# Which queue issues which of the first weight rows: two early transfers swapped between SyncE and ScalarE in a two-problem attention kernel

## The chip, the cores and the metric

The kernel runs on one core of a Trainium2 chip. The metric is the device time of one execution in microseconds (us), lower is better. Times are medians of several executions. Five engines matter: TensorE (PE, with its weight loader PEld), VectorE (DVE), ScalarE (ACT), GpSimd (POOL) and SyncE (SP). SyncE and ScalarE both issue memory transfers, each to a queue of its own; the profile calls the transfers of SyncE q1 and those of ScalarE q10.

## The reference

Two independent problems A and B of the same shape, each an attention block with cached keys and values; their outputs are laid side by side.

```python
# x (16,32,1024)  k_cache, v_cache (16,4,512,128)  wq (1024,4096)  wo (4096,1024), all bf16
q = (x @ wq).reshape(B, Sq, Hq, Dh).transpose(0, 2, 1, 3)
k = jnp.repeat(k_cache, rep, axis=1)
v = jnp.repeat(v_cache, rep, axis=1)
p = softmax(jnp.einsum("bhqd,bhkd->bhqk", q, k) * Dh ** -0.5)
o = jnp.einsum("bhqk,bhkd->bhqd", p, v)
out = o.transpose(0, 2, 1, 3).reshape(B, Sq, Hq * Dh) @ wo
```

## The kernel before

Only the opening, some 18 us of it, concerns the change. It computes the first eight heads of q for problem A. The rows of wq come in eight chunks of 128 rows (`dc` 0 to 7); w0 holds them for heads 0 to 7, and NF is 6, so "heads 0 to NF" are the six heads computed first. Chunks 0 and 1 of x come as rows and are transposed by TensorE; the others come by a transposing transfer.

```python
load_x(TT // 2, TT, nc.scalar)                 # half of x's rows, ScalarE
nc.scalar.preload_act_table_set("natural_log_exp_and_others")
load_x(0, TT // 2)                             # the other half, SyncE
load_w0(0, 1, 0, NF // 2)                      # chunk 0, heads 0 to 2, SyncE, 96 KB
load_w0(0, 1, NF // 2, NF)                     # chunk 0, heads 3 to 5, SyncE, 96 KB
load_w0(1, 2, 0, NF, nc.scalar)                # chunk 1, ScalarE, 192 KB
load_x_transposed(2)                           # chunks 2 and 3 of x, SyncE, 256 KB
load_w0(2, 3, 0, NF, nc.scalar)                # chunk 2, ScalarE, 192 KB
load_w0(3, 4, 0, NF)                           # chunk 3, SyncE
...
warm_up(22)                                    # dummy matmuls until x is there
for k, ts in enumerate(((0, TT // 2), (TT // 2, TT))):
    transpose_x(0, *ts, nc.vector.tensor_copy)
    transpose_x(1, *ts, nc.scalar.copy, spare[k])
for ts in ((0, TT // 2), (TT // 2, TT)):
    first_heads(range(0, NF // 2), (0,), *ts)  # six half-width matmuls
first_heads(range(NF // 2, NF), (0,))          # chunk 0, heads 3 to 5
first_heads(range(NF), (1, 2, 3))              # chunks 1, 2, 3
...
```

The prediction counts the chunks from one: its "first chunk" is chunk 0, its "second" chunk 1, its "third" chunk 2. I do the same below.

## Time and profile before

| | kernel before |
|---|---|
| median, three runs at first | 343.48 us |
| span of the profiled execution | 340.8 us |
| TensorE busy | 99% of the span |
| first matmul on the first weights (line 531) | 4.20 us |
| first matmul of the rest (line 301) | 18.45 us |

The page draws the span in 40 slices; a digit is the busy share in tenths, and PEclk is the granted TensorE clock in tenths. This is that part of the page of the kernel before:

```profile
PE   8999999999999999999999999999999999999996
...
PEclk9999999999999999999999999999999999999999
DMA  8999999989996998899999966998449996430001
```

### The profile page before, as it was taken

The page shows a single profiled execution, that of the slowest core. Times are in us where ns is not written, and L with a number is a line of the kernel's source. Part 1 is how long each engine was busy: PE and PEld are TensorE (multiplying, and loading weights), DVE is VectorE, ACT ScalarE, POOL GpSimd, SP SyncE. Part 2 cuts the span into 40 slices and gives each one's busy share as a digit, 9 for nine tenths or more (in the row PEclk, how much of TensorE's full clock was granted, in tenths as well). Part 3 has the DMA queues.
Part 4 walks back from the last instruction along what each step waited for, and adds up shares of the span by engine and source line. Part 5 has one row for each costly group of instructions (what it writes and reads, how often), then busy time and mean ns, then how long its engine had stood idle before and what let it go on. Part 6 is the DMA issues. An engine that isn't in the chain of part 4 may idle for free.

```text
span 340.8 us, 5475 instructions
## 1 busy us (share of the span) xinstructions
PE 336.7 (99%) x2113; PEld 213.0 (62%) x2113; DVE 265.2 (78%) x335; ACT 185.4 (54%) x208; POOL 46.7 (14%) x206
## 2 busy tenths in 40 slices
PE   8999999999999999999999999999999999999996
PEld 5456666666666666666666666666666666666555
DVE  0047988888888898888888898879888888889540
ACT  2067666666757667666645544554554555555110
POOL 0001111011111111110012221222122101111100
PEclk9999999999999999999999999999999999999999
DMA  8999999989996998899999966998449996430001
GB/s 208 297 186 270 287 248 223 188 238 259 312 266 159 241 230 227 214 291 296 317 297 285 239 125 148 344 283 211 125 106 300 355 193 161 105 100 13 17 19 33
DMA packets 128622, 71.70 MB, mean 210 GB/s; under 512 B 76880, under 2 KB 127824, under 8 KB 128592
## 3 DMA queue, kind: packets, MB, share of 16 engines
q1 hardware_dynamic: 127504, 69.68, 84.1%
q0 software_dynamic: 384, 1.05, 0.9%
q10 hardware_dynamic: 704, 0.59, 0.6%
q8 instruction: 17, 0.28, 0.4%
q14 instruction: 13, 0.11, 0.1%
HBM read 50.59 MB, written 2.10 MB: 155 GB/s over the span
## 4 chain that ended last, share of the span: by engine, by line
PE 99%; ACT 0%; issue 0%; ACTq 0%
PE f_ps L320 32%; PE q_ps L301 28%; PE s_ps L357 16%; PE ob L425 16%; PE q_ps L531 4%; PE q_ps L513 1%; PE xT_ps L521 0%; ACT o_sb L329 0%; ACTq L329 0%
## 5 line engine op out<-in xcount | busy, mean ns | idle before, releaser
L365 ACT ACTIVATE p_sb<-s_ps,shift 128x1024 bf16<-128x1024 f32 x128 | 142.7, 1115 | 97.5 <-PE s_ps L357 85.0
L376 DVE TRANSPOSE_TENSOR_REDUCE parts<-p_sb 128x32 f32<-128x1024 bf16 x128 | 158.8, 1240 | 20.9 <-ACT p_sb L365 19.3
L320 PE MATMUL f_ps<-wo_sb,oT 128*128 128x512 bf16 (+1 forms) x544 | 132.3, 366 | 0.0
L301 PE MATMUL q_ps<-xT,wq_sb 128*128 128x512 bf16 x448 | 116.9, 379 | 0.0
L357 PE MATMUL s_ps<-qT,kT 128*128 128x256 bf16 x512 | 76.8, 273 | 0.0
L425 PE MATMUL ob<-p_sb,v_sb 128*128 128x256 bf16 x512 | 76.8, 273 | 0.0
L320 PEld LDWEIGHTS <-oT 128*128 128x128 bf16 x544 | 53.2, 98 | 35.3
L357 PEld LDWEIGHTS <-kT 128*128 128x128 bf16 x512 | 56.9, 113 | 28.3
L301 PEld LDWEIGHTS <-wq_sb 128*128 128x128 bf16 x448 | 43.8, 98 | 32.2
L425 PEld LDWEIGHTS <-v_sb 128*128 128x128 bf16 x512 | 50.1, 98 | 20.0
L447 DVE TENSOR_TENSOR oT<-r,ob 128x512 bf16<-128x512 f32 x64 | 43.9, 686 | 19.9 <-PE ob L425 19.4
L411 DVE STREAM_TRANSPOSE r<-rall 128x512 f32<-128x512 f32 x64 | 44.2, 691 | 1.1
L309 ACT CAST qT<-q_ps 128x512 bf16<-128x512 f32 x56 | 32.7, 583 | 16.5 <-PE q_ps L301 16.5
L394 POOL COPY half<-cs 64x32 f32<-64x32 f32 x32 | 6.5, 204 | 231.4 <-DVE cs L384 231.3
L329 ACT CAST o_sb<-f_ps 128x512 bf16<-128x512 f32 (+1 forms) x17 | 9.5, 559 | 23.6 <-PE f_ps L320 23.6
L531 PE MATMUL q_ps<-xT,w_sb 128*128 128x512 bf16 (+1 forms) x67 | 14.4, 374 | 0.0
L384 DVE TENSOR_REDUCE cs<-parts 128x32 f32<-128x128 f32 x32 | 12.0, 376 | 1.1
L406 DVE RECIPROCAL rall<-sums 128x32 f32<-128x32 f32 x32 | 10.2, 320 | 3.3 <-POOL sums L403 3.3
L553 DVE CAST qT<-q_ps 128x512 bf16<-128x512 f32 x4 | 2.5, 684 | 12.8 <-PE q_ps L531 12.8
L531 PEld LDWEIGHTS <-w_sb 128*128 128x128 bf16 x67 | 6.5, 100 | 7.5 <-DMA w_sb<-in_A_wq_dram 0.3
L553 ACT CAST qT<-q_ps 128x512 bf16<-128x512 f32 x4 | 2.1, 599 | 12.3 <-PE q_ps L531 12.3
L331 POOL DMA_DIRECT2D out_dram<-o_sb x8 | 4.6, 574 | 29.3 <-ACT o_sb L329 29.3
(25 smaller groups left out, 48.2 us busy)
## 6 DMA issues: line engine op xcount, KB each, us to landing
v_sb<-in_A_v_cache_dram SPq DMA_DIRECT2D x16, 512.0 KB, 6.0
wq_sb<-in_B_wq_dram SPq DMA_DIRECT2D x8, 1024.0 KB, 5.8
wo_sb<-in_A_wo_dram SPq DMA_DIRECT2D x8, 1024.0 KB, 7.6
v_sb<-in_B_v_cache_dram SPq DMA_DIRECT2D x16, 512.0 KB, 4.8
wo_sb<-in_B_wo_dram SPq DMA_DIRECT2D x8, 1024.0 KB, 8.5
wq_sb<-in_A_wq_dram SPq DMA_DIRECT2D x5, 1024.0 KB, 6.7
wq_sb<-in_A_wq_dram SPq DMA_DIRECT2D x2, 512.0 KB, 7.3
kT<-in_A_k_cache_dram SPq DMA_TRANSPOSE x64, 4.4
```

The lines of the kernel that those rows point to most:

```text
L301: nc.tensor.matmul(ps[:], lhsT=w[:, dc, (h % 4) * DH:(h % 4 + 1) * DH], rhs=xT[pr][:, dc, :], start=(dc == 0), stop=(dc == DC - 1),)
L309: nc.scalar.copy(out=qT[pr, g][:, :, hl, :], in_=ps[:].rearrange("p (b s) -> p b s", s=SQ),)
L320: nc.tensor.matmul(ps[:, 0:width], lhsT=oT[pr, tt][:, h, :], rhs=wo_tiles[pr, nh, h // REP][:, h % REP, off:off + width], start=(h == 0), ...
L357: nc.tensor.matmul(s_ps[:, c, :], lhsT=kT[:, i % GRP, c, :], rhs=qT[pr, g][:, b, :, :].rearrange("p h s -> p (h s)"), start=True, stop=True,)
L365: nc.scalar.activation(out=p_sb[:], in_=s_ps[:], func=ACTF.Exp, bias=shift[:], scale=SCALE)
L376: nc.vector.tensor_reduce(out=parts[k][:, q, :, :].rearrange("p c h -> p (c h)"), in_=st[i]["p"][:].rearrange("p c (h s) -> p (c h) s", s=SQ),
L384: nc.vector.tensor_reduce(out=cs[:], in_=parts.pop(k)[:].rearrange("p q c h -> p q h c"), axis=AX.X, op=ALU.add,)
L406: nc.vector.reciprocal(out=rall[:, k, :], in_=quad.pop(k)[:])
L411: nc.vector.transpose(out=r[:].rearrange("p n s -> p (n s)"), in_=rall[:, k, o * 2 * REP:(o + 1) * 2 * REP] .unsqueeze(2).to_broadcast([P, ...
L425: nc.tensor.matmul(ob[j][:, q, :], lhsT=v_sb[:, i % GRP, c, :], rhs=st[i]["p"][:, c, :], start=(c == 0), stop=(c == KC - 1),)
L447: nc.vector.tensor_tensor(out=out, in0=rcp.pop(j)[:].rearrange("p (q h) s -> p q h s", h=REP), in1=ob.pop(j)[:].rearrange("p q (h s) -> p ...
L531: nc.tensor.matmul(first_q[h][:, ts], lhsT=w0[dc // HC][:, dc % HC, h * DH:(h + 1) * DH], rhs=xT[0][:, dc, ts], start=(dc == 0 and t0 == 0 ...
```

## The change

Its intent is to bring the first chunk's heads 3 to 5 earlier, as TensorE waits for them. They go to ScalarE's queue as its second transfer, and the second chunk takes their place on SyncE's. The third chunk stays ScalarE's third transfer; only its line in the program moves ahead of the transpose.

```diff
             load_x(0, TT // 2)
             load_w0(0, 1, 0, NF // 2)
-            load_w0(0, 1, NF // 2, NF)
-            load_w0(1, 2, 0, NF, nc.scalar)
+            load_w0(0, 1, NF // 2, NF, nc.scalar)
+            load_w0(1, 2, 0, NF)
+            load_w0(2, 3, 0, NF, nc.scalar)
             load_x_transposed(2)
-            load_w0(2, 3, 0, NF, nc.scalar)
             load_w0(3, 4, 0, NF)
```

## The prediction

> **What bounds the kernel now.** I read the page first, then the chain of waits, the waits of the weight loader, and the timeline and DMA views of the first 20 us.
>
> ```profile
> span 340.8 us, 5475 instructions
> PE 336.7 (99%) x2113; PEld 213.0 (62%) x2113; DVE 265.2 (78%) x335; ACT 185.4 (54%) x208; POOL 46.7 (14%) x206
> ...
> PE 99%; ACT 0%; issue 0%; ACTq 0%
> ```
>
> These are the span, the busy times and the chain that ended last, by engine. TensorE is 99% of that chain. A change that touches neither the number nor the shape of the matmuls can only win from the holes between them, and all of its edit lies before the 10th microsecond. The chain of waits for the first 25 us shows that opening (start, length, what):
>
> ```profile
> 0.93 2.52 PE q_ps L513 x22
> 3.45 0.95 PE xT_ps L521 x8
> 4.40 0.84 PE q_ps L531 x6
> 5.24 0.01 issue
> 5.25 13.36 PE q_ps L531 x61
> 18.61 3.45 PE q_ps L301 x16
> ```
>
> Warm-up matmuls run till x lands, eight transposes follow, then six half-width matmuls (first chunk, heads 0 to 2, two halves) and 61 full-width ones. The waits of the weight loader say where this stretch has holes:
>
> ```profile
> PEld L531 <- DMA w_sb<-in_A_wq_dram: 0.3, 1, 0.3
> PEld L521 <- DMA x_sb<-in_A_x_dram: 0.2, 1, 0.2
> ```
>
> Only the first of them, one wait for a weight transfer, is the target of this change. A loader runs ahead of the matmuls, so its 0.3 us is not TensorE's hole. The timeline of 5.0 to 5.23 us on TensorE gives that:
>
> ```profile
> 4.75 0.49 PE L531 MATMUL q_ps<-xT,w_sb 128*128 128x256 bf16 x3
> ```
>
> Three matmuls of 256 columns start at 4.75 and then 0.11 apart, so the third starts at 4.97 and TensorE could go on at 5.08. The chain has the next one (first chunk, head 3) at 5.25. **The hole is 5.25 - 5.08 = 0.17 us**, 0.05% of the span.
>
> The second thing to read is what follows it. From 5.25 three matmuls of the first chunk (heads 3 to 5) and six of the second come before the third chunk's first. The records place the starts of those nine 0.216 us apart (0.227 once), which makes 5.25 + 9 x 0.216 = 7.19, plus 0.01. The third chunk's first matmul starts at 7.23. It waits 0.03 us for the transposed rows of x (line 468), whose landing the DMA view of 2 to 4 us gives beside the weights' (KB each, us from issue to landing):
>
> ```profile
> w_sb<-in_A_wq_dram ACTq DMA_DIRECT2D x1, 192.0 KB, 4.3
> w_sb<-in_A_wq_dram SPq DMA_DIRECT2D x1, 192.0 KB, 4.4
> w_sb<-in_A_wq_dram SPq DMA_DIRECT2D x1, 96.0 KB, 3.5
> xT<-in_A_x_dram SPq DMA_TRANSPOSE x1, 5.0
> ```
>
> The timeline has the issues at: first chunk heads 0 to 2 on SyncE 1.25, second chunk on ScalarE 1.34, first chunk heads 3 to 5 on SyncE 1.75, third chunk on ScalarE 1.83, transpose on SyncE 2.22, fourth chunk on SyncE 3.60. With the times to landing (exact ones from the semaphore records) they land at 4.16, 5.01, **5.20**, 6.11, **7.19** and 7.96. So two landings hold TensorE, the one at 5.20 and the one at 7.19, and they are in series: the second has been almost met already.
>
> **What the Trainium skill says.** Its page "DMA: Bandwidth & Descriptors", section "Issuing engines are not separate DMA queues", says that transfers started by ScalarE and SyncE end up on the same 16 engines and that a second issuer only saves issue time. The trace agrees: both queues together move 276 GB/s in the stretch 2 to 4 us and 293 in 6 to 8 us with the engines near full, and the packets of the six transfers begin in the order of issue, whichever queue they are on (3.1, 3.4, 3.6 to 3.9, 4.1, 4.7, 6.3 us). So what the change alters is the order of transfers in one common line. The same page, "Queues, rings and completion order", says that an engine with work on two rows takes a packet of each in turn; the trace shows that too, with packets of both queues alternating from 3.4 to 5.6 us. "Perfetto Trace Analysis", section "DMA Instruction — HWDGE (DVE, Sync)", says that the data movement is not in the instruction's profiled window: here an issue lasts 0.43 us and the data lands 3.5 us after it, so I go by landings. "TensorE: Matmul & The Clock Gate", section "Wait — 56ns, not 53.3ns?", gives 215.7 ns between warm 512-column matmuls; the trace has 216 ns, so between the two landings TensorE can't be sped up.
>
> **The change, part by part.** No instruction is added or removed; three issues change their queue or place. The built program shows the same PE, DVE and POOL streams, with two semaphores swapped on TensorE.
>
> 1. *First chunk, heads 3 to 5: from SyncE's third issue to ScalarE's second.* Issued at 1.34 instead of 1.75, 0.41 us earlier, and 192 KB fewer stand ahead of it. Its rate is about 300 GB/s, so 192 KB are 0.64 us. I expect it to land 0.6 to 0.9 us earlier, near 4.4 (5.20 less 0.8, an estimate from these two numbers). Needed at 5.08. **The hole of 0.17 us closes.**
> 2. *Second chunk: from ScalarE's second issue to SyncE's third.* Issued 0.41 us later, with 96 KB more ahead (0.32 us). Where the two overlap on the line the sum of bytes is the same as that which landed at 5.20 before, so I put it at 5.2 to 5.6, the higher value if it shares the engines packet by packet with the third chunk's 192 KB. It is needed at 5.08 + 3 x 0.216 = 5.73. Cost nothing, with 0.1 to 0.5 us to spare.
> 3. *Third chunk: ScalarE's third issue as before*, at about 1.8. It lands between 5.6 and 6.1, and is needed at 5.08 + 9 x 0.216 = 7.02. Cost nothing.
> 4. *The transpose: still SyncE's fourth issue, at about 2.22.* The same bytes stand ahead of it (x, two parts of chunk one, chunks two and three), so I leave its landing at 7.19, with 0.2 us either way since it now follows a larger transfer in its own ring and has less beside it on the other. TensorE now wants it at 7.02 and gets it at 7.19: **a wait of 0.17 + 0.03 = 0.20 us here takes the place of the 0.17 + 0.03 us before**, and the third chunk starts at 7.23 as it did.
> 5. *All that comes after*: issued behind the transpose, in the same order, at the same times. The fourth chunk lands at 7.96 and is wanted at 7.23 + 5 x 0.216 = 8.31 by the loader, so it has 0.35 us to spare.
>
> Sum: -0.17 at 5.08, +0.17 at 7.02, so about 0.0 us. The time stays at the median before, 343.48; I write 343.4, as a transpose landing a little earlier would be paid out in full.
>
> **The rivals.**
> - *The transpose lands earlier too.* It doesn't carry the same work beside it, and if its packets got started before 4.7 us, up to all of the 0.20 us would be won: 343.28. Against it: the same bytes ahead, and in the trace its 1024 packets run in two halves (4.7 to 5.85, 5.9 to 6.4 us), the second starting when the slowest engine has finished the first. Weight packets on the other queue set that, and they are all still there.
> - *The second chunk becomes the wait.* If it shares packet by packet with the third chunk, and both end at 6.0, TensorE waits 0.3 us at 5.73, which then is inside the wait at 7.02 only in part: chunk two would start at 6.03, end at 7.33, 0.1 later than the landing of the transpose, so +0.1 us: 343.6. Against it: SyncE's issue (1.75) is still ahead of ScalarE's third (1.83), and so far packets began in order of issue.
> - *The transpose lands later.* With both big weight transfers alternating, its ring is blocked till about 5.1 instead of 4.7, and its landing slips by up to 0.4: 343.9. For it: SyncE's ring now holds 192 KB rather than 96 KB before the transpose. Against it: the second half then meets no weight packets, and the first half has fewer.
> - *A hole re-throttles TensorE.* The clock record has 1.00 throughout, and holes of 0.2 us were there before. I give it nothing.
>
> **Range and chances.** All mechanisms lie within -0.2 to +0.5 us. The three runs before spread from 342.94 to 343.48, and the profiled execution was another at 342.66, so the spread of measurement (0.8 us) is larger than all of them. Hence 342.7 to 344.0. A change of 2% would be 6.9 us; nothing in the first ten microseconds is that long. Chances: 0.005 faster, 0.99 same, 0.005 slower.
>
> **What would show the steps right or wrong.** In the profile after, the chain of waits should have the first chunk's heads 3 to 5 follow the six half-width matmuls at about 5.08, with no "issue" piece between them, and the loader's wait for w_sb at that place gone (step 1). The second chunk should start within 0.05 us of 5.73 (step 2), the loader showing no wait there. A hole of about 0.2 us should stand before the third chunk's first matmul, put down to the transposed x, with that matmul at 7.2 to 7.3 (step 4). The line 301 matmuls should again start at 18.6, give or take 0.2. I am wrong in the mechanism if they start at 18.4 (the transpose moved forward) or at 18.8 and later (it or the second chunk moved back), and wrong altogether if the time leaves 342.7 to 344.0 while the opening is unchanged, for then something outside it moved.

## The result

| | before | changed |
|---|---|---|
| median of 6 runs | 343.27 us | 342.91 us |
| lowest to highest | 342.94 to 343.48 | 342.55 to 343.21 |
| ratio | | 0.999, 95% interval 0.9977 to 1.0003 |
| span of the profiled execution | 340.8 us | 341.1 us |

A ratio is the mean time of one kernel's runs over that of the other's in the same rounds, so it is not quite the ratio of the medians. Executions over 1.5% slower than the fastest of the same kernel are left out of the means. The interval contains 1: the time is the same. The profiled execution of the changed kernel even has the longer span.

These lines of the changed kernel's page are the span, the busy times and the chain that ended last by engine:

```profile
span 341.1 us, 5436 instructions
...
PE 334.5 (98%) x2074; PEld 212.8 (62%) x2113; DVE 265.4 (78%) x335; ACT 185.3 (54%) x208; POOL 47.0 (14%) x206
...
PE 96%; DMA 2%; issue 1%; ACT 0%; SPq 0%; ACTq 0%
```

Before, TensorE had 99% of the chain; now it has 96%, and transfers have 2%. The matmul count of 2074 against 2113 is no change of work: the loader still has 2113 instructions, and 39 matmul records are missing from this trace. The chain bridges such gaps with pieces of "issue", which explains most of that 1%. The 2% of transfers is real, and the chain of waits in order of time shows where (start, length, what):

```profile
1.75 4.48 DMA w_sb<-in_A_wq_dram
6.23 0.05 issue
6.28 2.33 PE q_ps L531 x10
```

The waits of the loader and of TensorE in the same profile:

```profile
PEld L531 <- DMA w_sb<-in_A_wq_dram: 1.1, 1, 1.1
...
PE q_ps L531 <- DMA w_sb<-in_A_wq_dram: 0.6, 1, 0.6
```

There is still one wait for weights, and it is longer than the 0.3 us before. The transfer that ends it was issued at 1.75 us: that is SyncE's third issue, now the second chunk. The DMA view of 2 to 4 us (KB each, us to landing) has the transfers issued about then:

```profile
w_sb<-in_A_wq_dram SPq DMA_DIRECT2D x2, 192.0 KB, 4.5
w_sb<-in_A_wq_dram ACTq DMA_DIRECT2D x1, 192.0 KB, 4.7
xT<-in_A_x_dram SPq DMA_TRANSPOSE x1, 5.2
```

The semaphore records give the landings exactly; in them each transfer reports in sixteen completions, and the last one is its landing. The first chunk's heads 3 to 5 landed at 4.32 us (5.20 before), the second chunk at 6.23 (5.01), the third at 6.50 (6.11), the transposed x at 7.39 (7.19). TensorE's timeline from 5.3 to 5.9 us, and from 6.2 on:

```profile
5.09 0.59 PE L531 MATMUL q_ps<-xT,w_sb 128*128 128x512 bf16 x2
...
6.28 0.39 PE L531 MATMUL q_ps<-xT,w_sb 128*128 128x512 bf16 x1 [0.59 <-DMA w_sb<-in_A_wq_dram]
```

The last matmul of the first chunk starts at 5.30 and the next one could start 0.216 us later, at 5.52. It starts at 6.28: a hole of 0.76 us where the prediction had none. The old hole is gone: the six half-width matmuls and heads 3 to 5 follow each other from 4.17 on.

One more reading makes the rest simple. These are the line views of the kernel before (first and last start of a line's matmuls), for the first line after the opening and the last line of all:

```profile
L301 PE MATMUL q_ps<-xT,wq_sb x448: 379/379/379, 18.4 to 168.6; 128*128 128x512 bf16 x150
...
L320 PE MATMUL f_ps<-wo_sb,oT x544: 272/379/379, 169.3 to 337.4; 128*128 128x512 bf16 x160, 128*128 128x256 bf16 x22
```

and of the changed kernel:

```profile
L301 PE MATMUL q_ps<-xT,wq_sb x430: 379/379/379, 18.8 to 169.0; 128*128 128x512 bf16 x144
...
L320 PE MATMUL f_ps<-wo_sb,oT x524: 272/379/379, 169.6 to 337.8; 128*128 128x512 bf16 x154, 128*128 128x256 bf16 x21
```

From the first start of line 301 to the last start of line 320 it is 319.0 us in both; the instruction records say 318.957 us, and say so in all fourteen profiles, whatever was edited. **In these profiles, what happens in the opening is handed on in full, and nothing varies from there to the last start of line 320.** The end of the span follows that start by 3.35 to 3.37 us in thirteen of them and by 3.79 in one (the split second chunk, below). So the start of line 301 is the measure of an opening: 18.45 us before, 18.80 changed.

### The profile page after: what moved, and what is told of

Same layout as the page of the kernel before. It is cut to its first block, busy times and chain, and to the rows that moved or that the text cites. A ratio compares the mean times of both kernels' runs of the same rounds, so it can differ in the third digit from the quotient of the medians.

```text
span 341.1 us, 5436 instructions
## 1 busy us (share of the span) xinstructions
PE 334.5 (98%) x2074; PEld 212.8 (62%) x2113; DVE 265.4 (78%) x335; ACT 185.3 (54%) x208; POOL 47.0 (14%) x206
## 4 chain that ended last, share of the span: by engine, by line
PE 96%; DMA 2%; issue 1%; ACT 0%; SPq 0%; ACTq 0%
PE f_ps L320 31%; PE q_ps L301 28%; PE ob L425 17%; PE s_ps L357 16%; PE q_ps L531 4%; DMA w_sb<-in_A_wq_dram 1%; DMA out_dram<-o_sb 0%; ACT o_sb L329 0%; SPq L465 0%; SPq L474 0%; ACTq L329 0%; ACT p_sb L365 0%; ACTq L365 0%
## 5 line engine op out<-in xcount | busy, mean ns | idle before, releaser
L320 PE MATMUL f_ps<-wo_sb,oT 128*128 128x512 bf16 (+1 forms) x524 | 127.6, 366 | 0.6
L301 PE MATMUL q_ps<-xT,wq_sb 128*128 128x512 bf16 x430 | 113.0, 379 | 0.6
```

What stands on the lines that cost most here:

```text
L301: nc.tensor.matmul(ps[:], lhsT=w[:, dc, (h % 4) * DH:(h % 4 + 1) * DH], rhs=xT[pr][:, dc, :], start=(dc == 0), stop=(dc == DC - 1),)
L320: nc.tensor.matmul(ps[:, 0:width], lhsT=oT[pr, tt][:, h, :], rhs=wo_tiles[pr, nh, h // REP][:, h % REP, off:off + width], start=(h == 0), ...
```

## The experiments

The first theories after the result were three. *Held*: the transpose, once it moves, holds back the completions of weight transfers still in flight, because seven of the second chunk's sixteen completions came together at 6.14 to 6.23 us, just when the waiting packets of the transpose went on (6.11). (Its packets run in two halves: those of the first that are still open end together, and then the second half starts.) *Sharing*: the second chunk now has the third beside it on the other queue, both take turns, and both end late. *Chance*: single stalled reads, which fall on one transfer or another.

The experiments ran in three sessions, each on one chip: the second looks, the plain load and "ScalarE takes three" on chip 3; the third look at the kernel before, the late transpose, the first look with the third chunk on SyncE and the split chunk on chip 4; the rest on chip 14.

### Both kernels again

No edit; more profiles and times of each.

> The kernel before, unchanged: what a difference of nothing looks like, and a second profile of its opening. All theories: ratio within 0.1% of 1. Opening as in the first profile: the second chunk lands near 5.0 us (5.01 there) and is not waited for, a hole of about 0.17 us before head 3 of the first chunk, the third chunk's first matmul within 0.1 us of the transpose's landing (7.19 there). If the opening scatters by chance from execution to execution (the chance theory), the second chunk's landing moves by 0.5 us or more between the two profiles.

Measured: 343.71 us, ratio 1.0009 (0.9979 to 1.0040). The second chunk landed at 4.89. The hole before head 3 was 0.23 us, since that transfer landed at 5.64 and not at 5.20. The transposed x landed at 6.84 and was not waited for; the third chunk began at 7.64.

> The changed kernel, unchanged: a second profile. In the first, the second chunk's sixteen completions came at 4.47 to 5.04 (nine of them) and at 6.14 to 6.23 (seven), and TensorE stood 0.76 us. Shadow theory (a weight transfer that is still in flight when the transposed x begins to move completes only when the first half of the transpose has moved): again some completions at 6.1 to 6.3 and a hole of 0.5 to 0.8 us before the second chunk. Sharing theory (the second and third chunk take turns on the engines, so both end late): a landing at 5.5 to 6.2, without a jump between two groups. Chance theory (one stalled execution): a landing near 5.1 and no hole. Time within 0.15% of the kernel before under all three, since clock warm-up and holes scatter by some 0.3 us.

Measured: 343.03 us, ratio 0.9984 (0.9958 to 1.0009). The second chunk landed at 6.26, again with a group of eight at 6.14 or later. The hole, though, was only 0.19 us. The chain of waits in this profile:

```profile
4.30 1.98 PE q_ps L531 x9
6.28 0.03 issue
6.31 12.69 PE q_ps L531 x58
```

The landing was as late as before, and yet TensorE was busy almost until then: the same nine matmuls whose first and last starts were 1.13 us apart in the first profile (4.17 to 5.30) started from 4.10 to 5.90 here, 1.80 us apart. The spacing is 0.213 us for 256 columns, against 0.108 us in the first profile. **TensorE ran at half rate** until about 5.6 us. So a late landing costs what remains of it after a slow TensorE.

> The kernel before once more, for a third profile of its opening and for more times of it beside the others. All theories: hole before the first chunk's head 3 of 0.1 to 0.6 us (0.17 and 0.23 in the first two), none before the second chunk, 0 to 0.1 before the third; second chunk landed by 5.1. Ratio within 0.15% of 1.

Measured: 343.44 us, ratio 1.0017 (0.9990 to 1.0044). The second chunk landed at 4.88. Heads 3 to 5 of the first landed at 5.67, and yet the hole was 0.03 us, because TensorE was at half rate until about 6.0 us and came to them only at 5.69. The expectation of at least 0.1 us failed for that reason.

> The changed kernel, a third look. The second chunk lands at 6.1 to 6.3 (6.23 and 6.26 before). The hole before it depends on when TensorE's matmuls change from 0.43 to 0.216 us spacing: 0.6 to 0.8 us if that is before 4.9 us, 0.1 to 0.4 if it is between 5 and 6, none if later. Time 0 to 0.2% under the kernel before, and no execution over 344.5, where the kernel before had 6 of 40 near 345.2.

Measured: 343.33 us, ratio 0.9995 (0.9981 to 1.0009). The second chunk landed at 5.03 this time, in one group, and TensorE was at half rate until after 6.7 us, so there was no hole for data at all. Line 301 still started at 19.27, the latest of the six profiles. The chain of this profile, and the stretches 5.43 to 6.70 and 7.19 to 8.48 us on TensorE (length, busy time with the matmuls that touch the stretch, granted clock, DMA share, GB/s):

```profile
4.36 4.72 PE q_ps L531 x19
```

```profile
5.43:6.70 1.27, 1.27 (x4) 1.00 1.17 238
7.19:8.48 1.29, 1.29 (x7) 1.00 1.08 337
```

Stretches of equal length have four matmuls and seven; the starts are 0.427 and 0.216 us apart. The granted clock reads 1.00 in both, so this view does not show the half rate. The record behind it does: in the packed trace of this profile the first clock record begins at 6.80 us, just where the spacing changes, and the view counts time without a record as full.

The six openings together, from the instruction, semaphore and clock records. The full rate begins with the first clock record. A hole is a spacing of two starts less the spacing at the rate of the moment:

| profile | heads 3-5 land | 2nd chunk lands | full rate from | holes for data | line 301 starts |
|---|---|---|---|---|---|
| before, 1st | 5.20 | 5.01 | 4.6 | 0.17 + 0.03 | 18.45 |
| before, 2nd | 5.64 | 4.89 | 5.3 | 0.23 | 18.87 |
| before, 3rd | 5.67 | 4.88 | 6.0 | 0.03 | 19.00 |
| changed, 1st | 4.32 | 6.23 | 4.0 | 0.76 | 18.80 |
| changed, 2nd | 4.64 | 6.26 | 5.6 (no record; by spacing) | 0.19 | 18.84 |
| changed, 3rd | 4.49 | 5.03 | 6.8 | none | 19.27 |

The means of the last column are 18.77 and 18.97 us, with a spread of half a microsecond inside each kernel. The moment of full rate scatters by 2.8 us (4.0 to 6.8) and shows no tie to the change; at half rate half of that time is lost. The clock records at full rate last 337.919 us in six of the profiles and 334.506 us in seven, which is 99 and 98 times 3.413 us: as if the rate changed on a fixed beat of 3.413 us and the kernel's start fell anywhere in it. That is argued from these lengths and not tested.

### Without the transpose

```diff
-            load_x_transposed(2)
+            nc.sync.dma_start(
+                out=xT[0][:, 2:4, :],
+                in_=A_x.flatten_outer_dims()[0:P, :].rearrange("p (d n) -> p d n", d=2),
+            )
```

> The changed kernel with its first transposing transfer of x replaced by a plain load of as many bytes (256 KB) into the same tile, in the same place of SyncE's order. The result is wrong on purpose. Shadow theory: without a transpose in flight all sixteen completions of the second chunk come by 5.3, without a gap between two groups, the third chunk lands by 5.9, and the hole before the second chunk is gone. Sharing theory: both chunks still take turns and the second lands at 5.5 or later, so a hole of 0.1 to 0.7 us stays. Time not over 0.25% below the kernel before.

Measured: 343.27 us, ratio 0.9988 (0.9955 to 1.0021). It passed the comparison with the reference although a quarter of x was wrong for every head of problem A (all of them read this tile); that says something of the tolerance only. The second chunk landed at 6.66, its completions spread from 4.34 to 5.73 with one more at 6.66, and the hole before it was 0.69 us. The chain names it:

```profile
1.75 4.91 DMA w_sb<-in_A_wq_dram
```

The held theory wanted all completions by 5.3. It falls as the cause: without any transpose in flight the second chunk was later still, though by one completion of the sixteen. The packets of the changed kernel say the same: the chunk's last data packet ended at 5.80 and 5.79 us in the first two looks and at 4.68 in the third, so what is late is the data and not only the report.

```diff
-            load_x_transposed(2)
             load_w0(3, 4, 0, NF)
+            load_x_transposed(2)
```

> The changed kernel with the first transpose moved behind the fourth chunk; the second and the third chunk still share the line from two queues. Held theory: with no transpose moving before about 5.8, the second chunk's completions come without a jump between two groups, all by 5.6, and the third's by 6.0. Sharing theory: the second lands at 5.5 or later as before, so 0 to 0.7 us of hole stay. Transposed x lands later, at 7.5 to 8.2, and TensorE waits for it 0.4 to 1.1 us before the third chunk. Time 0 to 0.3% over the changed kernel.

Measured: 343.64 us, ratio 1.0003 (0.9978 to 1.0028). The second chunk landed at 6.23, its completions spread from 4.62 on without a group at the end:

```profile
w_sb<-in_A_wq_dram SPq DMA_DIRECT2D x1, 192.0 KB, 4.5
```

That is against the held theory as the cause once more: the jump belongs to the transpose, the lateness does not. The hold itself is there, though. Here no weight completion came between 6.42 and 7.00 us, and then sixteen came by 7.27, as the first half of the transposed x ended at 6.97 to 7.02. In each of the thirteen profiles with this transpose, 7 to 19 weight completions came between the end of its first half and 0.25 us later, and at most two in the 0.4 us before. The transposed x landed at 8.24 and cost 0.23 us, less than expected, because TensorE was at half rate until about 6.8.

### The third chunk behind the second, on the same queue

```diff
-            load_w0(2, 3, 0, NF, nc.scalar)
+            load_w0(2, 3, 0, NF)
```

> The changed kernel with the third chunk moved to SyncE, right behind the second chunk and ahead of the transpose; ScalarE then issues only x's half and the first chunk's heads 3 to 5. So nothing shares the line with the second chunk from the other queue once the first chunk is through, and the bytes ahead of the transpose stay the same. Sharing theory: the second chunk lands at 4.7 to 5.3 in one group, no hole before it (needed at about 5.7); the third at 5.4 to 6.0; transposed x near 7.2. Held theory (completions still open when the transpose starts are held till its first half is through) says the same of the second chunk, as it is done before the transpose starts, and holds the third at about 6.1. Chance theory (single reads stall for up to 1 us, whichever transfer they belong to): a straggler in the second chunk stays, 5.5 or later. Time 0 to 0.2% under the changed kernel if the hole goes.

Measured: 342.97 us, ratio 0.9983 (0.9962 to 1.0005). The second chunk landed at 5.15 in one group, the third at 5.83, the transposed x at 6.85. No hole for data. The DMA view around its issue at 1.75, and the chain:

```profile
w_sb<-in_A_wq_dram SPq DMA_DIRECT2D x1, 192.0 KB, 3.4
```

```profile
4.30 4.27 PE q_ps L531 x19
```

The same transfer, issued at the same 1.75 us on the same queue, took 3.4 us to land where it had taken 4.5.

> The best arrangement so far (third chunk on SyncE behind the second), unchanged, a second look. Sharing theory: second chunk again lands in one group by 5.3 (5.15 in the first look), third by 6.0, transposed x near 6.9, so no hole for data after the first matmul on w_sb, whatever the clock does. Chance theory: a straggler past 5.5. Time 0 to 0.3% under the kernel before, within 0.1% of the changed kernel.

Measured: 342.88 us, ratio 0.9994 (0.9979 to 1.0008). Second chunk 5.14, third 6.04, transposed x 7.10, no hole; line 301 started at 18.56 (18.77 in the look before).

```diff
-            load_w0(1, 2, 0, NF)
-            load_w0(2, 3, 0, NF, nc.scalar)
+            load_w0(1, 2, 0, NF // 2)
+            load_w0(1, 2, NF // 2, NF, nc.scalar)
+            load_w0(2, 3, 0, NF)
```

> As the run with the third chunk on SyncE, but the second chunk is cut in two: SyncE issues its heads 0 to 2, ScalarE its heads 3 to 5. Each half is 96 KB. If a transfer's landing is set by the bytes ahead of it in both queues together, the halves land at 4.6 to 5.2, the third chunk at 5.5 to 6.1, transposed x near 7.2: no hole before the second chunk. If single stalled reads decide it, the halves scatter as the whole did (one of them past 5.5). Time equal to the run with the third chunk on SyncE within 0.1%.

Measured: 343.61 us, ratio 1.0000 (0.9980 to 1.0021). The halves landed at 4.93 and 5.11, the third chunk at 5.70, the transposed x at 6.74: no hole, as expected. It is 0.19% slower than its neighbour of the same session (343.61 over 342.97), where I had expected 0.1%; its profile was at half rate until about 7.0 us and ended 0.43 us later than the others after the last start of line 320, and with medians of five executions I can't tell an effect of the edit from that.

### ScalarE takes three

```diff
-            load_w0(1, 2, 0, NF)
+            load_w0(1, 2, 0, NF, nc.scalar)
```

> One part of the change alone: ScalarE issues the first chunk's heads 3 to 5 first and then both the second and the third chunk, SyncE goes from the first chunk's heads 0 to 2 straight to the transpose. The first chunk should land near 4.3 as in the changed kernel, so the hole of 0.17 us closes. The transpose is issued at 1.75 instead of 2.22, beside the second chunk and ahead of the third. Shadow theory: the second chunk completes only with the first half of the transpose, which is earlier too, near 5.3, and the third chunk later, near 6.0; the hole before the second chunk is 0 to 0.3 us. Sharing theory: the second chunk has only the transpose beside it and lands near 5.1, no hole. Transposed x lands 0.3 to 0.8 us before 7.19. Time 0 to 0.2% below the kernel before.

Measured: 344.64 us, ratio 1.0027 (0.9993 to 1.0061). The first chunk's heads 3 to 5 landed at 4.38 as expected. The second chunk, now beside the transpose on the other queue, landed at 6.51, later than either theory had it. All sixteen completions came at 6.40 to 6.51, after the end of the transpose's first half (6.10 to 6.21), as the held theory has it; but its last data packet had ended only at 6.15. And the third chunk was the surprise. The chain:

```profile
0.82 3.03 DMA x_sb<-in_A_x_dram
...
3.87 5.46 DMA w_sb<-in_A_wq_dram
```

ScalarE's fourth transfer got the completion semaphore of x's half, its first one, and so was not issued before that half had landed at 3.85. Two microseconds late and behind SyncE's next transfers, it landed at 9.33, and TensorE stood 1.27 us. Line 301 started at 20.61, which is 1.6 to 2.2 us after the three profiles of the kernel before (18.45 to 19.00), and the span was 342.9 against 340.8, 341.2 and 341.3. A delay in the opening is paid at the end in full.

### The rate and the hole

On the kernel with the third chunk on SyncE:

```diff
-            warm_up(22)
+            warm_up(11)
```

> The third chunk on SyncE, with 11 warm-up matmuls in place of 22: TensorE stands idle from about 2.1 us till x lands near 3.2. No landing changes. Clock theory (the opening's end is set by the moment TensorE gets its full rate as much as by landings, and that moment follows sustained work): full rate comes later than the 4.2 to 6.8 us seen so far, at 6.5 to 10, and the time rises by 0.4 to 2 us over the same kernel with 22. If landings alone set the end: no change beyond 0.3 us.

Measured: 343.61 us, ratio 1.0016 (1.0002 to 1.0030), 0.7 us over the same kernel with 22 on the same chip (342.88). In its profile full rate came at about 6.2 us, inside the range seen with 22 and not beyond it, so this one look does not show the expected later moment. That the dummy matmuls are worth something is suggested by the time and not shown: the interval is against the kernel before, which differs in more, and the five executions with 11 (343.12 to 344.39) overlap the five with 22 (342.65 to 343.43). That they would be worth it through an earlier full rate is argued.

On the kernel before:

```diff
+            warm_up(4)
             first_heads(range(NF // 2, NF), (0,))
```

> The kernel before with four dummy matmuls of 128 columns (0.22 us at full rate, 0.43 at half) in the place of the hole before the first chunk's head 3; they write a bank that head 3 overwrites. Landing theory: the hole is filled with work that counts for nothing, and all else stays: time within 0.1% of the kernel before, with 0 to 0.2 us added when the clock is at half rate. Clock theory for the slow executions near 345.2 us (the hole spoils the sustained work that the clock waits for): none of these among its executions, which with 5 of them would be a hint and no proof. If the hole has nothing to do with them, about one in seven again.

Measured: 343.44 us, ratio 0.9997 (0.9982 to 1.0011), highest 343.50. In the profile heads 3 to 5 landed at 6.13, later than in any profile of the unedited kernel, and TensorE, at full rate from 4.0 us, stood from the last dummy until 6.18. The chain:

```profile
1.75 4.38 DMA w_sb<-in_A_wq_dram
```

So SyncE's third transfer can be late in the old arrangement too: 5.20, 5.64, 5.67 and now 6.13 us. And here the hold has a part: nine of the sixteen completions of heads 3 to 5 came at 6.02 to 6.13, right after the end of the transposed x's first half (5.97 to 6.00), though their last data packet, too, had ended only at 5.64. It is plainer in the second look at the kernel before, where the last data packet ended at 4.87 and nine completions came only at 5.53 to 5.64, after that half (5.50 to 5.53). In the first profile the transfer was complete well before the half ended (5.91), and it landed 0.38 us after its last data packet.

### What stays open

Six of the 48 fast executions of the kernel before took 344.97 to 345.57 us, and none of the 17 of the changed kernel passed 343.60. All six came in two of the four sessions, on two chips. No profile fell on one of them, so I don't know what they are, nor whether the change removes them: only 6 of its 17 executions ran in these two sessions. The kernel with the hole filled was to give a hint and gave none, as no execution of its session was slow in this way, the kernel before included. One further execution of the kernel before took 727.32 us, about twice the usual; it was not profiled either.

## Why the prediction was right or wrong

**The time.** 343.4 was predicted with 342.7 to 344.0, and 342.91 measured. Over all 17 executions of the changed kernel the median is 342.97 us, over the 48 fast ones of the kernel before 343.31. That is 0.1%, and the three intervals (0.9977 to 1.0003, 0.9958 to 1.0009, 0.9981 to 1.0009) all contain 1. The forecast "same" was right; a gain of about 0.3 us may be there and is not shown.

**What bounds the kernel.** Right, and firmer than I had it: 318.957 us after the opening in every profile.

**Step 1, heads 3 to 5 land near 4.4 and the hole closes.** Right: 4.32, 4.64 and 4.49 us, none waited for. Its value was read from one lucky profile, though. The hole was 0.17, 0.23 and 0.03 us in three profiles of the kernel before, and what it is depends on the rate of TensorE.

**Step 2, the second chunk lands at 5.2 to 5.6 and costs nothing.** This is the step that failed. It landed at 6.23 and 6.26 in two looks of three (5.03 in the third). I had written that the sum of bytes ahead is what counts. What the runs showed in its place is a landing 0.6 us above that range in two looks of three; they point to what travels on the other queue beside it. With the third chunk beside it on ScalarE's queue it was at 6.23 or later in four profiles of five (the changed kernel three times, the plain load, the late transpose). With the third chunk behind it on its own queue it was at 5.15, 5.14 and 4.83 us (the last with 11 warm-ups), and its split halves were at 5.11 and before. With the transpose beside it, 6.51. Nine profiles against chance is not a proof, and chance has its part, as the 5.03 shows. The chip is a rival that was not tested: on chip 14 the changed kernel's 5.03 stands beside 5.14 and 4.83, so there the company made no difference; on chip 3 there are late profiles alone; within one chip only the late transpose (6.23) against 5.15 and the split halves (5.11), on chip 4, speaks for it. So the cause is likely and not shown. What happened in two looks of three is the second of the prediction's rivals, "the second chunk becomes the wait" with both ending "at 6.0". Its argument against, that packets begin in the order of issue, was true and beside the point: what is late is the end. On the trace, single 1536-byte packets of the second chunk took up to 0.87 us in the late looks at the changed kernel (nine of them over 0.2 us in each) where 0.065 is usual; its third look has one such packet, of 0.32, but the first look with the third chunk on SyncE has several, up to 0.58, and landed early. Why they stall is open.

**Step 3, the third chunk costs nothing.** Right in its cost: 6.50, 6.46 and 5.64 us, needed after the second chunk's six matmuls. Its range of 5.6 to 6.1 was short by 0.4.

**Step 4, a wait of 0.20 us for the transposed x takes the place of the old one.** Wrong in form. In no profile of the changed kernel did TensorE wait for it. It landed at 7.39, 7.38 and 6.90 us, and TensorE came to the third chunk at 7.58, 7.61 and later, held up by the second chunk or by its own half rate. The wait that took the place of the old one stood one chunk earlier and was up to 0.76 us.

**Step 5, all after it at the same times.** Right for the sequence: no later hole in any of the profiles of the two kernels.

**The sum.** -0.17 + 0.17 was to be zero. In the first pair of profiles it is -0.17 - 0.03 for the old holes, +0.76 for the new one, and -0.2 for an earlier full rate and a start 0.02 earlier: +0.36, which is what the starts of line 301 differ by (18.80 less 18.45, rounded). In the second pair the holes are 0.23 and 0.19, in the third 0.03 and none, as the half rate hides most of them. So the sum was near zero for a reason that the prediction did not have.

**The rival that I gave nothing.** "A hole re-throttles TensorE. The clock record has 1.00 throughout." The view that I read is no evidence for the opening: it says 1.00 while the spacing of matmuls is twice what it is later, because the first clock record begins only with the full rate, at 4.64 us in that profile. I had the numbers before me (the first two spacings on line 531 in the profile before are 0.206 and 0.214 us for 256 columns, the later ones 0.11) and took only the late ones. That a hole takes the full rate away again can be ruled out for holes of this size: TensorE, once at full rate, stood 0.76 us in the changed kernel, 1.0 us with the hole filled and 1.27 us with ScalarE taking three, and in all thirteen profiles that have clock records the one at full rate runs on past the last matmul. Whether a hole before it delays the full rate was not settled.

**The gain that was sought.** The arrangement with the third chunk on SyncE has neither hole and the best pair of medians, 342.97 and 342.88 us. Its ratios of 0.9983 and 0.9994 have intervals that contain 1, so it can't be said to beat either kernel. An opening without holes for data is left with the half rate. Sixty-seven matmuls at full rate would take 6 x 0.109 + 61 x 0.216 = 13.83 us; the start of line 301 less the first start on line 531, less 13.83 and less the holes, leaves 0.04 us for it in the first profile of the changed kernel and 1.30 in the third.

## What to carry to other kernels

When two queues feed a tight opening, moving a transfer earlier moves another one beside new company; look at the landing of each transfer in several profiles, and try what is needed soon without a large transfer issued at the same moment on the other queue (here likely the cause, not proved). Look also whether a needed transfer is still open when the first half of a transpose is about to end: here its last completions then came in a group just after that half. Before counting a hole of 0.2 us, look whether the engine is at its full rate there: a hole that a slow engine covers is worth nothing. And find the stretch that never varies: here 318.957 us after the opening, which turned a question of 0.1% in the time into one of 0.4 us in one start.

## What the Trainium skill lacked or had wrong

- "TensorE: Matmul & The Clock Gate", section "What you observe", puts the change to full rate around 4 us into sustained matmuls, give or take 0.5 us, with the spacing about halved. The spacing agrees (0.213 us for 256 columns, then 0.109), but the moment was 4.0 to 7.0 us in the profiles, 3.0 to 6.0 us after the first matmul at 0.93, a spread of 3.0 us. (The work here is not the page's plain row of matmuls: eight transposes and a short wait for x lie in it.)
- No page says that the profile's granted clock counts the time before the first clock record as full: it read 1.00 in a stretch with starts 0.427 us apart and in one with 0.216, while the record began between them, at 6.80 us.
- "DMA: Bandwidth & Descriptors", section "Issuing engines are not separate DMA queues", says that a second issuer only saves issue time, as all transfers interleave on the same engines. It doesn't say how far a neighbour on the other queue may put off a landing: 6.23 us or later in four profiles of five with the next chunk on ScalarE's queue, 4.83 to 5.15 with it behind on SyncE's (a difference of chips is not ruled out).
- No page has the two halves of a DMA transpose: in the changed kernel's trace nine packets of the transposed x that began at 5.14 to 5.84 us stayed open and all ended at 6.11 to 6.13, and weight transfers that were still open then completed together just after it (6.14 to 6.23). The late transpose shows the same at 6.97 to 7.02 us, and so do all thirteen profiles with this transpose.
